# Batch 1's attention in two row parts, and only the unused slots of P's buffers cleared

## The chip, the cores and the metric

The kernel runs on one core of a Trainium2 chip. The metric is the device time of one execution in microseconds (us); of several runs of a kernel the median is given. A core has five engines with queues of their own: TensorE (PE; "PEld" in the profile is its loading of weights), VectorE (DVE), ScalarE (ACT), GpSimd (POOL) and SyncE (SP). SP issues all DMAs of this kernel, in the order of its queue.

## What is computed

Causal attention over 4 batches, 12 heads, 448 tokens and 64 dimensions, all in float32; its output, laid out as 1792 tokens by 768, goes through a multi-layer perceptron (MLP) with a squared ReLU:

```python
def _attn_ref(q, k, v):                     # (4, 12, 448, 64)
    scores = scale * np.matmul(q, k.transpose(0, 1, 3, 2))
    scores = np.where(mask, -1000000000.0, scores)
    scores = scores - np.max(scores, axis=-1, keepdims=True)
    attn = np.exp(scores)
    attn = attn / (np.sum(attn, axis=-1, keepdims=True) + 1e-09)
    return np.matmul(attn, v)

def _moe_ref(x, w_in, w_out):               # (1792, 768), (768, 2048), (2048, 768)
    r = np.maximum(x @ w_in, 0.0)
    return (r * r) @ w_out
```

## The kernel before

**Arithmetic.** The large products run in fp16: each operand is a sum of two fp16 halves, hi and lo, and a product is three fp16 products (hi·hi, hi·lo, lo·hi). The batches 0 and 1 have their scores in float32, the batches 2 and 3 in split fp16.

**Stages.** Batch 0's attention is computed first, while the weights arrive and are split (`early`, in two row parts of 256 and 192 tokens; `weights_in`, `weights_out`). Then, for each batch, `attention(b)` works on six pairs of heads (`pair`), and the MLP on blocks of up to 256 tokens (`sub_block`). Batch 0's MLP has blocks of 256 and 128 tokens; its last 64 tokens go with the first 192 of batch 1 into batch 1's first block (`segs` `[(64, 0), (192, 1)]` in the loop at the end of the kernel), and the following 256 tokens are batch 1's second block.

**A pair.** The rows of a head's scores are cut into four chunks of 112 (`NCH` = 4, `P` = 112); chunk c needs c + 1 chunks of k, so a head has 1 + 2 + 3 + 4 = 10 tiles of 112 x 112. For a pair of batch 1: q and k are loaded (L563, one DMA a head) and v (L567); they are turned on PE (L650) and copied back (L601); the scores are products (L700); VectorE masks and takes the row's maximum (L669), ScalarE takes exp with the sums (L673), VectorE the reciprocals (L710, L713). `halves` writes P's normalised hi (L453) and lo (L466) into the buffer `psrc`, of which there are two, one for each head of the pair. `psrc` has 26 slots of 128 x 128; a slot holds one tile of hi or lo, and six of the 26 hold none. One DMA transpose (L617) turns the 26 blocks into `pt`, from which the values are products (L724, 24 a pair) with v's halves; L736, L737 and L740 write x's hi and lo into `xt`. For batch 1 a copy on GpSimd (L744) brings the 64 tokens of batch 0 along.

**A block.** `sub_block` squares x (L1076, L1079), sums the columns by one product with ones (L1082), makes a power of two for each token from it (L1087 to L1093), rescales x (L1099, three instructions for six pairs), and multiplies with `w_in` (L1139, "L1": 16 groups of 18 products). ReLU, square and halves follow (L1150 to L1157, L453 to L466), then the products with `w_out` (L1176, "L2"), and the output (L1188, L1193, L1197). L1 needs x of all six pairs.

**The order.** Nothing is written in the order in which it runs: each operation is given to a planner (`Plan`) with its reads and writes, its engines (some may run on either of two) and a due time. The due time comes from the table `PR` (a base and a step for each stage, a shift for each kind). `order()` simulates the engines and takes on each the ready operation of the least due time; `elsewhere()` chooses between engines. The engines' queues then run in that fixed order.

**Clearing.** Slots of `psrc` that hold no tile are read by the DMA transpose all the same; `pads` (L1239) clears both buffers whole by GpSimd memsets (L1241) after the last use by batch 0's attention.

Of the kernel before, what the change touches and what calls it, by code (L numbers as in the profile page):

```python
# [1299 lines left out]
```

## Time and profile before

| | us |
|---|---|
| median of 3 runs | 653.37 |
| lowest, highest | 652.10, 654.14 |
| the profiled execution: its own time | 653.86 |
| its span from first to last instruction | 651.8 |
| TensorE's mean granted clock | 0.99 |

| engine | busy, us | share of the span |
|---|---|---|
| PE | 614.0 | 94% |
| DVE | 423.5 | 65% |
| ACT | 415.3 | 64% |
| POOL | 140.4 | 22% |

Times in the rows count from the start of the span. An entry "[2.78 <-DVE xt L1099]" in a timeline says that the engine was idle for 2.78 us before the instruction and what ended that: here a VectorE instruction of line 1099 that wrote xt. The granted clock is a share of TensorE's full 2.4 GHz.

### The profile page before, as it was taken

Reading aid. Unit: us, or ns where it says so; the run is one execution under the profiler, and the core shown is the slowest. Engines: PE = TensorE matmul, PEld = TensorE weight load, DVE = VectorE, ACT = ScalarE, POOL = GpSimd, SP = SyncE. Lnnn points to the kernel's source line nnn. Section 1 sums busy time; section 2 is a strip of 40 time slices with the busy share of each in tenths; the row PEclk is TensorE's granted clock in tenths of the full one; section 3 lists DMA queues with packets and bytes.
Section 4 is the critical chain, followed back from the end, with each engine's and each line's share of the span. In section 5 each row is a group of like instructions: output and inputs, shape, how many; then the busy total and the mean of one; then the engine's idle time right before and its main releaser. Section 6 shows DMA issues by size and latency. Waiting matters only on the chain.

```text
span 651.8 us, 14056 instructions
## 1 busy us (share of the span) xinstructions
PE 614.0 (94%) x5166; PEld 446.6 (69%) x5166; DVE 423.5 (65%) x1263; ACT 415.3 (64%) x1171; POOL 140.4 (22%) x200
## 2 busy tenths in 40 slices
PE   6887999969998996999999999999999999999997
PEld 3553778758664564887767866878768778767764
DVE  3989999999889856779787599885402511401100
ACT  3977999756999975888677799886213233104300
POOL 1000234768300000242004221144012132003300
PEclk9998999999999996999999999999999999999999
DMA  8993574546889897359975989987000000000000
GB/s 217 288 304 123 182 265 166 173 156 165 153 187 205 207 235 175 86 107 197 189 177 110 208 183 204 178 182 141 14 24 14 14 14 13 1 25 13 13 25 24
DMA packets 208771, 87.31 MB, mean 134 GB/s; under 512 B 196160, under 2 KB 203584, under 8 KB 208704
## 3 DMA queue, kind: packets, MB, share of 16 engines
q1 hardware_dynamic: 208704, 86.43, 54.8%
q8 instruction: 40, 0.66, 0.4%
q14 instruction: 27, 0.22, 0.1%
HBM read 45.81 MB, written 5.51 MB: 79 GB/s over the span
## 4 chain that ended last, share of the span: by engine, by line
PE 57%; issue 15%; DVE 14%; ACT 5%; DMA 5%; SPq 3%; POOL 1%; POOLq 0%; ACTq 0%; DVEq 0%
PE bank L1176 25%; PE bank L1139 23%; PE bank L724 3%; PE bank L686 3%; DMA pt<-psrc 2%; DVE wo L929 2%; DVE wo L926 2%; DVE wo L923 2%; SPq L756 1%; DVE bank L814 1%; DMA xt<-in_moe_w_in_dram 1%; DVE wi L929 1%; DMA g<-in_moe_w_in_dram 1%; DVE wi L926 1%; PE bank L938 1%
## 5 line engine op out<-in xcount | busy, mean ns | idle before, releaser
L1139 PE MATMUL bank<-xt,wi 128*128 128x256 f16 (+1 forms) x2304 | 234.7, 261 | 6.1 <-DVE xt L1099 5.2
L1139 PEld LDWEIGHTS <-wi 128*128 128x128 f16 x2304 | 201.7, 98 | 31.9 <-issue 7.7
L1176 PE MATMUL bank<-wo,g 128*128 128x384 f16 x1248 | 212.8, 326 | 0.2 <-DVE wo L466 0.2
L1176 PEld LDWEIGHTS <-g 128*128 128x128 f16 x1248 | 120.4, 98 | 80.4 <-issue 5.0
L461 POOL TENSOR_TENSOR g<-g,g 128x256 f16<-128x256 f32 (+1 forms) x112 | 78.6, 711 | 305.2 <-ACT g L453 174.9
L1152 DVE TENSOR_SCALAR r<-bank 128x256 f32<-128x256 f32 (+1 forms) x96 | 38.1, 400 | 92.5 <-PE bank L1139 61.7
L1157 ACT ACTIVATE g<-r 128x256 f32<-128x256 f32 (+1 forms) x128 | 48.8, 386 | 52.4 <-DVE r L1152 41.0
L673 ACT ACTIVATE pq<-bank,nm 112x336 f32<-112x336 f32 (+3 forms) x144 | 70.7, 508 | 17.0 <-DVE nm L669 10.7
L466 DVE SCALAR_TENSOR_TENSOR psrc<-pq,nm,psrc 112x224 f16<-112x224 f32 (+3 forms) x144 | 71.2, 526 | 5.9 <-ACT psrc L453 5.2
L1193 DVE SCALAR_TENSOR_TENSOR ob<-bank,fac,ob 128x384 f32<-128x384 f32 x26 | 16.0, 615 | 82.6 <-PE bank L1176 82.3
L453 ACT ACTIVATE psrc<-pq,nm 112x224 f16<-112x224 f32 (+3 forms) x144 | 65.3, 545 | 2.9 <-DMA pt<-psrc 2.9
L1188 ACT ACTIVATE ob<-bank,fac 128x384 f32<-128x384 f32 x26 | 15.1, 581 | 74.6 <-PE bank L1176 74.5
L453 ACT ACTIVATE g<-g 128x256 f16<-128x256 f32 (+1 forms) x96 | 36.2, 394 | 32.2 <-PE bank L1176 30.5
L669 DVE CUSTOM_DVE_ANT_0 bank<-bank,mask,sc 112x112 f32<-112x112 f32 (+3 forms) x96 | 46.2, 511 | 7.2 <-PE bank L686 6.1
L455 POOL TENSOR_SCALAR g<-g 128x256 f16<-128x256 f32 x16 | 14.9, 936 | 99.4 <-ACT g L1157 99.4
L686 PE MATMUL bank<-qk 128*112 128x112 f16 (+3 forms) x192 | 33.2, 290 | 3.2 <-DMA qk<-qk 2.9
L673 ACT ACTIVATION_READ_ACCUMULATOR pq<-bank,nm 112x1 f32 x144 | 31.5, 219 | 0.0
L724 PE MATMUL bank<-pt,vp 112*64 112x448 f16 (+3 forms) x432 | 29.9, 284 | 1.0 <-DMA pt<-psrc 0.9
L724 PEld LDWEIGHTS <-vp 112*64 112x64 f16 x432 | 21.8, 110 | 11.5 <-issue 6.1
L686 PEld LDWEIGHTS <-qk 128*112 128x112 f16 x192 | 20.8, 133 | 8.9 <-DMA qk<-qk 3.6
L806 PE MATMUL bank<-wo 64*96 64x256 f32 (+4 forms) x144 | 19.7, 382 | 4.4 <-ACT wo L601 4.3
L814 DVE CUSTOM_DVE_ANT_0 bank<-bank,mask 128x128 f32<-128x128 f32 (+3 forms) x48 | 21.3, 486 | 2.6 <-PE bank L806 2.4
(147 smaller groups left out, 802.0 us busy)
## 6 DMA issues: line engine op xcount, KB each, us to landing
raw<-in_moe_w_out_dram SPq DMA_DIRECT2D x8, 768.0 KB, 4.2
xt<-in_moe_w_out_dram SPq DMA_DIRECT2D x8, 768.0 KB, 4.8
xt<-in_moe_w_in_dram SPq DMA_DIRECT2D x11, 512.0 KB, 6.6
out_dram<-ob SPq DMA_DIRECT2D x26, 192.0 KB, 1.9
raw<-in_moe_w_in_dram SPq DMA_DIRECT2D x9, 512.0 KB, 7.5
vn<-in_v_dram SPq DMA_DIRECT2D x18, 224.0 KB, 3.4
raw<-in_v_dram SPq DMA_DIRECT2D x18, 224.0 KB, 3.1
raw<-in_q_dram SPq DMA_DIRECT2D x12, 224.0 KB, 3.2
```

The costliest lines, as they stand in the source:

```text
L453: nc.scalar.activation(out=o, in_=i, func=ACTF.Copy, scale=s)
L461: return plan.add({"dve": dve_ns(n), "pool": pool2_ns(n)}, lambda e: engines[e].tensor_tensor(out=out(), in0=in_(), in1=top(), op=ALU.subt ...
L466: nc.vector.scalar_tensor_tensor(out=out(), in0=in_(), scalar=scale(), in1=top(), op0=ALU.mult, op1=ALU.subtract)
L669: one("dve", dve_ns(w, 1, 2 if F16S[b] else 1) - 10, lambda e: nc.vector.tensor_tensor_reduce(out=s.ap[0:P, 0:w], in0=s.ap[0:P, 0:w], in1= ...
L673: one("act", act_ns(w, True, 1, True), lambda e: nc.scalar.activation(out=p32[j].ap[0:P, b0 * P:b0 * P + w], in_=s.ap[0:P, 0:w], func=ACTF ...
L686: nc.tensor.matmul(out=s.ap[0:P, 0:(c + 1) * P], lhsT=qT.ap[:, j * NCH + c, :], rhs=kT.ap[:, a:a + c + 1, :].rearrange("p a t -> p (a t)") ...
L724: nc.tensor.matmul(out=pv.ap[j * D:(j + 1) * D, kc * P:S], lhsT=vp.ap[:, hv, vb:vb + D], rhs=pT[j].ap[0:P, hp * NSL + x:hp * NSL + x + w, ...
L814: one("dve", dve_ns(w, 1, 1) - 10, lambda e, c=c, j=j, w=w, ss=ss, nm=nm: nc.vector.tensor_tensor_reduce(out=ss[j].ap[0:M, 0:w], in0=ss[j] ...
L1139: nc.tensor.matmul(out=h.ap[:, 0:n], lhsT=wi_hl(ci, hw)[:, ms], rhs=x[:, kd, hx, off:off + n], start=(kd == 0 and hw == 0 and hx == 0), st ...
L1152: nc.vector.tensor_scalar(out=r.ap[:, 0:n], in0=h.ap[:, 0:n], scalar1=0.0, scalar2=None, op0=ALU.max)
L1157: nc.scalar.activation(out=g32.ap[:, 0:n], in_=r.ap[:, 0:n], func=ACTF.Square)
L1176: nc.tensor.matmul(out=o.ap[:, 0:HALF], lhsT=gv[:, kf, hg, tt * 128:(tt + 1) * 128], rhs=wo_hl(kf, hw)[:, hh * HALF:(hh + 1) * HALF], star ...
```

## The change

1. **Batch 1's attention in two row parts.** `attention(1)` runs twelve jobs in place of six pairs: first all six pairs with the row chunks 0 and 1 (224 rows), then all six with the chunks 2 and 3. Batch 1's first MLP block needs the first part of x alone. The second part has a phase of its own in the table ("f", with F0 and FR). k's chunks 0 and 1 and v's are loaded, turned and split in both parts. A first-part job uses one half of each buffer of P, of `psrc` and of `pt` (by turns), and a DMA transpose of 6 blocks; a second-part job the whole, and 16 blocks (`SLOTS`).
2. **Clearing.** `pads` clears only the slots and the columns that hold nothing, by four ACT copies of zeros (or VectorE memsets) for each of the two buffers. The mask is cleared by VectorE.
3. **The table `PR`** has new values throughout, so that instructions move on every engine.

```diff
-    "B1": -5632767, "B2": -48927, "B3": -8054168, "E0": -8696670, "ER": 17110, "M0": 3904615, "N0": -9012245,
+    "B1": -4814806, "B2": 259207, "B3": -8361854, "E0": -9195508, "ER": 139465, "F0": -2935097, "FR": 16247,
...
-    def pair_load(i):
+    def pair_load(i, cs=tuple(range(NCH))):
         b, pr = divmod(i, NPAIR)
+        c0, c1 = cs[0], cs[-1] + 1
+        phase, at = ("f", 2 * pr) if c0 else ("a", 2 * i)
         for n, a in enumerate((q, k, v)):
             t, keys = raw_of(i)[n]
+            ca = 0 if n else c0
+            nc_ = c1 - ca
...
+    def halves(due, cs, src, skey, rr, rkey, ps, pT, pj):
+        first, step, ns = SLOTS[cs[0], len(cs)]
...
+        one("sp", 19.2 * 2 * ns, lambda e: nc.sync.dma_start_transpose(
+            out=pT.ap[:, 0:2 * ns], in_=ps.ap[0:P, 0:2 * ns].rearrange("p a d -> p (a d)")),
+            [(ps, c, z) for c in cs for z in range(2)] + [("pads", pj)], [pT], due, 260.0 + 125.0 * 2 * ns)
+
+    SLOTS = {(0, NCH): (0, NCH - 1, NSL), (0, 2): (0, 1, 3), (2, 2): (2, 2, 8)}
...
+                chunks = range(c0 * (1 - n), c1)
...
+        z = None if whole or c0 else pr % 2
+        p32, pT, ps = [[mk(j, z) for j in range(2)] for mk in (n_p32, n_pT, n_ps)]
...
         def values16(e):
-            for kc in range(NCH):
-                x, w = 4 * kc, NCH - kc
+            for kc in range(c1):
+                ca = max(kc, c0)
+                x, w = step * kc + ca - first, c1 - ca
...
-        xk = [("xt", b % 2, pr, z) for z in range(3)]
+        xk = [("xt", b % 2, pr, z) for z in ((1, 2) if c0 else (0, 1) if not whole else range(3))]
...
+        if b == 1:
+            jobs = [(i, cs) for cs in ((0, 1), (2, 3)) for i in pairs]
+            for x, job in enumerate(jobs):
+                for n in jobs[x + (x > 0):x + 2]:
+                    pair_load(*n)
+                pair(job[0], None, job[1])
+            return
...
-        nc.gpsimd.memset(mask, 0.0)
+        nc.vector.memset(mask, 0.0)
...
-    def pads(e):
-        for t in psrc:
-            nc.gpsimd.memset(t, 0.0)
+    def pads(e, t):
+        for w in (t[:, :, P:], t[:, 6:15:8, 0:P], t[:, 20:21, 0:P], t[:, 23:25, 0:P]):
+            if e == "act":
+                nc.scalar.activation(out=w, in_=mask[0:P, 0:w.shape[2]].unsqueeze(1).to_broadcast(list(w.shape)), func=ACTF.Copy)
+            else:
+                nc.vector.memset(w, 0.0)
...
-    spare = [plan.spot([("psrc", i, j) for j in range(2)], psrc[i]) for i in range(2)]
-    plan.add({"pool": 2000}, pads, [], spare + ["pads"] + [("psrc", i, c, z) for i in range(2) for c in range(NCH) for z in range(2)],
-             ("a", H, "ld"))
+    for j in range(2):
+        plan.add({"dve": 900, "act": 1250}, lambda e, t=psrc[j][0:P]: pads(e, t), [], [n_ps(j), ("pads", j)], ("a", H, "ld"), "pad", True)
```

In the changed kernel the lines have other numbers: L1210 is L2 (L1176 before), L1116 the column sums (L1082), L1173 L1 (L1139), L731 the fp32 scores (L700), L758 the values (L724), L677 the turning of q and k (L650), L638 the DMA transpose (L617), L579, L585 and L589 the loads (L563, L567), L1283 the clearing.

TensorE where batch 0's MLP ends, before: the last L2 products, the column sums of batch 1's first block, its first L1 products.

```order
L1176 LDWEIGHTS qk
L1176 MATMUL bank_123<-wo,qk 128x384
L1176 LDWEIGHTS qk
L1176 MATMUL bank_123<-wo,qk 128x384
L1082 LDWEIGHTS ones_b
L1082 MATMUL bank_119<-sq,ones_b 128x256
L1139 LDWEIGHTS wi
L1139 MATMUL bank_123<-xt_143,wi 128x256
L1139 LDWEIGHTS wi
L1139 MATMUL bank_123<-xt_143,wi 128x256
```

After, at the same place: the column sums, then work of a second-part job.

```order
L1210 LDWEIGHTS qk
L1210 MATMUL bank_123<-wo,qk 128x384
L677 MATMUL bank_111<-ident,raw 128x112 x4
L1116 LDWEIGHTS ones_b
L1116 MATMUL bank_119<-sq,ones_b 128x256
L731 MATMUL bank_115<-raw 112x336
L731 MATMUL bank_131<-raw 112x336
L731 MATMUL bank_107<-raw 112x448
L731 MATMUL bank_111<-raw 112x448
L758 LDWEIGHTS vp
```

Further on, the first L1 products of the block stand behind the scores of the last second-part job:

```order
L758 LDWEIGHTS vp
L758 MATMUL bank_103<-pt,vp 64x112
L677 MATMUL bank_115<-ident,raw 128x112 x2
L677 MATMUL bank_131<-ident,raw 128x112 x4
L731 MATMUL bank_107<-raw 112x336
L731 MATMUL bank_111<-raw 112x336
L731 MATMUL bank_115<-raw 112x448
L731 MATMUL bank_131<-raw 112x448
L1173 LDWEIGHTS wi
L1173 MATMUL bank_123<-xt_143,wi 128x256
```

What moved: 24 values, turns and scores now stand between the column sums and L1, and L1's first 18 products stand ahead of the values of the last three second-part jobs (two more groups of 24 follow further down, the last one behind 144 products of L1).

SP in batch 1's attention, before: one pair's loads and the two DMA transposes of 26 blocks.

```order
L617 DMA_TRANSPOSE pt<-psrc_145 128x26x112
L617 DMA_TRANSPOSE pt<-psrc_146 128x26x112
L563 DMA raw<-in_q_dram 112x4x64 x2
L563 DMA raw<-in_k_dram 112x4x64 x2
L567 DMA raw<-in_v_dram 112x8x64
L617 DMA_TRANSPOSE pt<-psrc_145 128x26x112
L617 DMA_TRANSPOSE pt<-psrc_146 128x26x112
```

After, in the second part: the transposes have 16 blocks (in the first part 6).

```order
L638 DMA_TRANSPOSE pt<-psrc_145 128x16x112
L638 DMA_TRANSPOSE pt<-psrc_146 128x16x112
L579 DMA raw<-in_q_dram 112x2x64 x2
L579 DMA raw<-in_k_dram 112x4x64 x2
L589 DMA raw<-in_v_dram 112x8x64
L638 DMA_TRANSPOSE pt<-psrc_145 128x16x112
L638 DMA_TRANSPOSE pt<-psrc_146 128x16x112
```

What moved: as many loads stand between two jobs of the second part as stood between two pairs (q's for half the rows, k's and v's for all), and there are six jobs of the first part besides.

The clearing, before, on GpSimd, between the halves of batch 0's MLP:

```order
L455 TENSOR_SCALAR g<-g_1529 128x256
L461 TENSOR_TENSOR g<-g_1529,g 128x256
L1241 MEMSET psrc_145 128x3328
L1241 MEMSET psrc_146 128x3328
L455 TENSOR_SCALAR g<-g_1595 128x256
L455 TENSOR_SCALAR g<-g_1612 128x256
```

After, on ACT; the same four copies for psrc_146 follow some fifteen rows later.

```order
L1191 ACTIVATE g_1478<-r 128x256
L1283 ACTIVATE psrc_145<-mask 112x26x16
L1283 ACTIVATE psrc_145<-mask 112x2x112
L1283 ACTIVATE psrc_145<-mask 112x112
L1283 ACTIVATE psrc_145<-mask 112x2x112
L615 ACTIVATE psrc_146<-psrc_146,nm 96x352 x2
L1184 ACTIVATE r<-bank_119 128x256
L531 ACTIVATE junk,vst<-vn 128x448
```

What moved: the clearing has left GpSimd's queue for ACT's, and it stands before the end of batch 0's attention (L615 is a normalisation of that).

## Rows read from the trace of the kernel before

**Rows 1.** The page: busy us (share of the span) xinstructions of each engine.

```profile
PE 614.0 (94%) x5166; PEld 446.6 (69%) x5166; DVE 423.5 (65%) x1263; ACT 415.3 (64%) x1171; POOL 140.4 (22%) x200
```

**Rows 2.** Windows: in each stretch, busy us of each engine, PEclk, DMA share, GB/s.

```profile
66.00:120.00 54.00, 54.00 (x512) 43.19 (x511) 52.22 (x125) 52.35 (x135) 19.88 (x20) 1.00 0.54 188
120.00:160.00 40.00, 32.95 (x428) 29.14 (x427) 39.76 (x72) 22.62 (x64) 30.89 (x34) 1.00 0.62 188
160.00:245.00 85.00, 80.87 (x623) 48.23 (x621) 70.72 (x223) 78.93 (x227) 8.76 (x19) 1.00 0.89 194
245.00:261.00 16.00, 9.87 (x56) 6.67 (x54) 10.41 (x37) 8.97 (x27) 0.67 (x1) 0.68 0.75 171
```

**Rows 3.** PE's timeline, 241 to 261 us: start, length, engine, line, operands, [idle before <-releaser].

```profile
241.64 4.07 PE L1176 MATMUL bank<-wo,qk 128*128 128x384 f16 x24
245.80 0.27 PE L1082 MATMUL bank<-sq,ones_b 128*128 128x256 bf16 x1
248.85 0.81 PE L1139 MATMUL bank<-xt,wi 128*128 128x256 f16 x6 [2.78 <-DVE xt L1099]
250.46 1.44 PE L1139 MATMUL bank<-xt,wi 128*128 128x256 f16 x6 [0.79 <-DVE xt L1099]
...
256.08 1.09 PE L686 MATMUL bank<-qk 128*112 128x336 f16 x5 [2.30 <-DMA qk<-qk]
256.96 3.51 PE L1139 MATMUL bank<-xt,wi 128*128 128x256 f16 x18
```

**Rows 4.** VectorE's timeline, 248 to 252 us: first and third rescaling.

```profile
248.12 0.68 DVE L1099 TENSOR_TENSOR xt<-xt,sg 128x1024 f16<-128x1024 f16 x1
...
251.32 0.68 DVE L1099 TENSOR_TENSOR xt<-xt,sg 128x1024 f16<-128x1024 f16 x1
```

**Rows 5.** The chain of waits: start, us, engine, what, line, instructions.

```profile
408.95 1.55 PE bank L724 x24
410.50 0.81 PE bank L686 x6
...
530.89 15.72 PE bank L1139 x144
```

**Rows 6.** PE's timeline, 188 us: eight turns of q and k.

```profile
188.05 1.01 PE L650 MATMUL bank<-ident,raw 112*128 112x112 f32 x8
188.89 2.12 PE L1176 MATMUL bank<-wo,g 128*128 128x384 f16 x12
```

**Rows 7.** Timelines of GpSimd, VectorE and PE, 125 to 135 us.

```profile
125.03 5.68 POOL L1241 MEMSET psrc<- 128x3328 f16 x2
...
126.13 4.99 DVE L923 TENSOR_SCALAR wo<-raw 128x768 int32<-128x768 int32 x1
...
134.46 0.55 DVE L923 TENSOR_SCALAR wo<-xt 128x768 int32<-128x768 int32 x1
...
131.23 0.51 PE L1015 MATMUL bank<-wo 128*128 128x128 bf16 x6 [2.23 <-DVE p L478]
```

**Rows 8.** Groups by line and form: ACT's normalisation of 448 columns.

```profile
L593 ACT ACTIVATE psrc<-psrc,nm 96x448 f32<-96x448 f32 x8 | 5.3, 664 | 0.0
```

**Rows 9.** PE's timeline, first and last of five waits in 160 to 240.

```profile
196.70 1.57 PE L700 MATMUL bank<-raw 64*112 64x336 f32 x6 [0.58 <-ACT pq L673]
...
227.87 1.59 PE L724 MATMUL bank<-pt,vp 112*64 112x448 f16 x23 [0.59 <-DMA pt<-psrc]
```

**Rows 10.** SP's timeline: DMA issues, 181 to 248 us.

```profile
181.33 6.37 SPq L617 DMA_TRANSPOSE pt<-psrc  x2
187.75 1.11 SPq L563 DMA_DIRECT2D raw<-in_q_dram  x2
...
246.57 1.23 SPq L636 DMA_TRANSPOSE qk<-qs  x1
```

**Rows 11.** DMA issues: operands, engine, count, KB each, median us to landing.

```profile
raw<-in_q_dram SPq DMA_DIRECT2D x12, 224.0 KB, 3.2
...
raw<-in_q_dram SPq DMA_DIRECT2D x12, 112.0 KB, 2.7
```

More of the change, by code (lines that the diff above doesn't have):

```diff
@@ L61 @@
+    "ws_wn.hi@act": -38135, "ws_wn.hi@dve": 129552, "ws_wn.hi@pool": 72402, "ws_wn.lo@dve": 16397,
+    "ws_wn.lo@pool": 120960, "ws_wn.rest@act": -91715, "ws_wn.rest@dve": 56998, "wt_wn": 1241781,
+    "wt_wn.hi@act": -289805, "wt_wn.hi@dve": 27877, "wt_wn.hi@pool": 117559, "wt_wn.lo@dve": 112951,
+    "wt_wn.lo@pool": -81617,
 }
@@ L404, in attention_relu2_kernel, with n_part @@
     pt = const.tile([128, 2, 2 * NSL * P], F16, name="pt")
-    n_p32 = lambda j: plan.spot([("pq", j, z) for z in range(2)], pq[:, j])
-    n_pT = lambda j: plan.spot([("pt", j, z) for z in range(2)], pt[:, j].rearrange("p (a t) -> p a t", t=P))
+    def n_part(tag, j, z, ap):
+        n = ap.shape[1] // 2
+        return plan.spot([(tag, j, x) for x in range(2) if z in (None, x)], ap if z is None else ap[:, z * n:(z + 1) * n])
+    n_p32 = lambda j, z=None: n_part("pq", j, z, pq[:, j])
+    n_pT = lambda j, z=None: n_part("pt", j, z, pt[:, j].rearrange("p (a t) -> p a t", t=P))
+    n_ps = lambda j, z=None: n_part("psrc", j, z, psrc[j])
     def n_ep(part, j, z):
@@ L679, in pair @@
             for j in range(2):
-                for c in range(NCH):
+                for c in cs:
                     s = n_s(b, 0)
@@ L690, in pair @@
                     one("pe", 2 * mm_ns((c + 1) * P), scores16, [qT, (kT, 0), (kT, 1), (kT, 2)], [s],
-                        ("a", 2 * i + j + 0.05 * c, "sc"))
+                        (phase, at + j + 0.05 * c, "sc"))
                     soft(c, j, s)
         else:
-            for c in range(NCH):
+            for c in cs:
                 ss = [n_s(b, j) for j in range(2)]
@@ L707, in pair @@
         for j in range(2):
-            due = ("a", 2 * i + j, "P")
+            due = (phase, at + j, "P")
             rr = lambda a, z, j=j: f32(nm[j], 4 + a, 4 + z)
             one("dve", 69, lambda e, j=j, rr=rr: nc.vector.tensor_scalar(
-                out=rr(0, NCH), in0=f32(sm[j], 0, NCH), scalar1=1e-9, scalar2=1.0 / PSC, op0=ALU.add, op1=ALU.mult),
-                [(sm[j], c) for c in range(NCH)], [(nm[j], "t")], due, port=True)
-            one("dve", 94, lambda e, rr=rr: nc.vector.reciprocal(out=rr(0, NCH), in_=rr(0, NCH)),
+                out=rr(c0, c1), in0=f32(sm[j], c0, c1), scalar1=1e-9, scalar2=1.0 / PSC, op0=ALU.add, op1=ALU.mult),
+                [(sm[j], c) for c in cs], [(nm[j], "t")], due, port=True)
@@ L714, in pair @@
+            one("dve", 94, lambda e, rr=rr: nc.vector.reciprocal(out=rr(c0, c1), in_=rr(c0, c1)),
                 [(nm[j], "t")], [(nm[j], "r")], due, port=True)
-            halves(n=2 * i + j, src=lambda j=j: p3(j), skey=p32[j], rr=rr, rkey=(nm[j], "r"), pT=pT[j])
+            halves(due, cs, src=lambda j=j: p3(j), skey=p32[j], rr=rr, rkey=(nm[j], "r"), ps=ps[j], pT=pT[j], pj=j)
         pv = n_pv(b)
+        first, step, ns = SLOTS[c0, len(cs)]
+        t0, t1 = c0 * P, c1 * P
         def values16(e):
-            for kc in range(NCH):
-                x, w = 4 * kc, NCH - kc
+            for kc in range(c1):
+                ca = max(kc, c0)
+                x, w = step * kc + ca - first, c1 - ca
@@ L721, in values16 @@
                 for z, (hv, hp) in enumerate(((0, 0), (0, 1), (1, 0))):
                     for j in range(2):
-                        vb = (j * NCH + kc) * D
+                        vb = (j * c1 + kc) * D
                         nc.tensor.matmul(
-                            out=pv.ap[j * D:(j + 1) * D, kc * P:S], lhsT=vp.ap[:, hv, vb:vb + D],
-                            rhs=pT[j].ap[0:P, hp * NSL + x:hp * NSL + x + w, :].rearrange("p a t -> p (a t)"),
-                            start=(kc == 0 and z == 0), stop=(kc == NCH - 1 and z == 2))
@@ L729, in pair @@
-        due = ("a", 2 * i + 1, "val")
-        one("pe", 1550, values16, [(vp, 0), (vp, 1)] + pT, [pv], due, tiled=True)
-        due = ("a", 2 * i + 1, "x")
+                            out=pv.ap[j * D:(j + 1) * D, ca * P:t1], lhsT=vp.ap[:, hv, vb:vb + D],
+                            rhs=pT[j].ap[0:P, hp * ns + x:hp * ns + x + w, :].rearrange("p a t -> p (a t)"),
+                            start=(kc == 0 and z == 0), stop=(kc == c1 - 1 and z == 2))
+        due = (phase, at + 1, "val")
+        one("pe", 3 * sum(mm_ns((c1 - max(kc, c0)) * P) + 10 for kc in range(c1)) + 15, values16, [(vp, 0), (vp, 1)] + pT, [pv], due, tiled=True)
@@ L742, in pair @@
             [pv] + xk, xk, due)
-        if b % 2:
+        if b % 2 and not c0:
             one("pool", pool_ns(128), lambda e: nc.gpsimd.tensor_scalar(
```

113 lines of the change are left out of this document (60 added, 53 removed), and 44 rows, old and new, of tables (LINES, PR).

## The prediction

> **What bounds the kernel now.** I began with the busy shares of the page: TensorE (PE) is busy 94% of the span, the others at most 65% [rows 1]. So the kernel loses time only where PE stands still or runs at half clock, and gains none from work taken off another engine unless PE was waiting for that engine. The second view is the table of stretches [rows 2]. From 66 to 120 us PE is busy 54.00 of 54 us. From 120 to 160 it is busy 32.95 of 40, beside a VectorE (DVE) that is busy 39.76: there DVE is the bound. From 160 to 245, the attention of batch 1, PE is busy 80.87 of 85, ScalarE (ACT) 78.93. From 245 to 261 PE is busy only 9.87 of 16 us, at a mean granted clock of 0.68: for its length the worst of these stretches.
>
> The third view is PE's timeline around that stretch [rows 3]. The last product of batch 0's second MLP half ends at 241.64 + 4.07 = 245.71. Then PE has the column sums for batch 1's first block (L1082, 0.27 us), and 2.78 us of nothing, until VectorE's rescaling (L1099) of that block's x; further waits of 0.79, 0.16 (not shown) and 2.30 us follow, the last one for batch 2's scores. The first 36 products of the block's L1 end at 256.96 + 3.51 = 260.47. VectorE's own timeline shows the chain [rows 4]: the first rescale starts at 248.12 and the third ends at 252.00. Nothing else is ready then: all of batch 0's work is used up, and every product of batch 1 needs this block.
>
> How much is lost? From 245.71 to 260.47 are 14.76 us. At full clock an L1 product costs 15.72 / 144 = 0.109 us, six fp16 scores 0.81 us [rows 5]; 36 products, six scores and the column sums (some 0.1) make 3.93 + 0.81 + 0.1 = 4.85 us. So **9.9 us** are lost, some 6 of them as idle time and the rest by products at half clock (1.2 GHz): L1's first six after the wait take 1.44 us from start to end [rows 3], against 0.65 at full clock.
>
> **The change, part by part.**
>
> *Batch 1 in two row parts.* The first 64 + 192 tokens of the MLP now need only the first 224 rows of batch 1, six jobs that are done before the six jobs of the second part. The order shows what that does: the column sums of the block stand right behind the last product of batch 0, but 24 value products, six transposes and eight fp32 scores of the second part stand between them and the first L1 product; and 144 products of L1 then stand ahead of the last value products. What stands between is about 1.55 us of values [rows 5], 0.6 of transposes (0.105 each, below) and 1.6 to 1.9 of scores, some 4 us, against 2.7 us from the column sums to the end of the first rescale (246.07 to 248.80). In VectorE's order the three rescales stand ahead of the masking of the following scores. So the wait has its cover, the clock has no reason to fall, and batch 0's last MLP work no longer has to fill the wait for batch 1's last values: L1 does. I take back 8.9 us of the 9.9 and leave 1 for the second and third rescale and for batch 2's first scores, whose 2.30 us wait is on their own DMA. Bounds: −9.9 to −7.0. If that cover were gone, the 2.78 us wait would come back first.
>
> *Added PE work.* The first two row chunks of k are transposed twice: 12 more transposes. Eight take 0.84 us from their start at 188.05 to the next instruction [rows 6], 0.105 each: +1.2 us. The value products grow from 24 to 12 + 24 for a pair, 72 more over six pairs, with the same number of columns in all. The trace has no product split this way. Free at one end; at the other each costs the mean 1.55 / 24 = 0.065 [rows 5], +4.7 us. I take +2.0, since the new ones are short ones. Together **+3.2** (+1.2 to +6.0).
>
> *The memsets.* Before, GpSimd clears both psrc buffers whole at 125.03 for 5.68 us; a VectorE instruction that starts beside it takes 4.99 us, and 0.55 for the same shape at 134.46; PE stands idle 2.23 us right after [rows 7]. Now eight ACT copies of zeros clear only the unused slots. By the nearest ACT row, a scaled copy of 448 columns, each costs at most 0.66 us, so at most 5.3 together on ACT [rows 8]. The order also takes 12 of the 48 normalisations of batch 0 from ACT to VectorE (10 rows, two of them double): ACT loses 12 x 0.6 = 7 us of work, VectorE takes on about 12 x 0.55 = 6.6, by its 768-column row [rows 7]. Thus VectorE gets 4.4 us back and some 6.6 more to do. Some of it lies in 66 to 120, where PE had no idle time to lose; some in VectorE's bound stretch. I take **−1.5** (−4.4 to +1.0). The Trainium skill (SBUF — State Buffer, "SBUF: two separate sides") says that a GpSimd instruction and a VectorE one in a two-port mode take the shared port pair as an exclusive lock, the other one waiting for the whole instruction; the 4.99 us agree with that. By this rule alone the 4.4 would all come back in a stretch that VectorE bounds, and the sum would be 2.9 lower.
>
> *Waits inside batch 1's attention.* PE waits five times there, 0.58 + 0.81 + 0.47 + 1.20 + 0.59 = 3.65 us in all, mostly for exp on ACT [rows 9]. Twelve shorter jobs in place of six have twice as many such places, but more MLP work to put between (L1 beside the last three jobs). Between −3.7 (all covered) and +4.0 (as many again) I take **−1.0**, since the same ACT work now spreads over a stretch that is longer by L1's share.
>
> *SP's queue.* SP issues all loads and DMA transposes in order. A transpose of 26 blocks occupies it 6.37 / 2 = 3.2 us, one of 8 blocks 1.23; a plain load 0.55 [rows 10]. On that line a block costs 0.11 and an instruction 0.35: 6 blocks 1.0, 16 blocks 2.1. Twelve of each take 37 us, as twelve of 26 do now. Loads of batch 1 grow from 30 to 66: +20 us at 0.55, in a stretch of some 100 us of which SP then uses about 80. Loads stand one job ahead in the order, so this costs nothing; a 112 KB load lands in 2.7 us and a 224 KB one in 3.2 [rows 11], so halving buys nearly nothing but delays nothing either. If that cover is gone, see the third rival.
>
> The sum: 653.86 (the profiled execution's own time: 651.8 of span and 2.06 outside) − 8.9 + 3.2 − 1.5 − 1.0 = 645.7. The profiled execution is 0.5 above the median of 653.37, so 645.2 for the median.
>
> **The rivals.**
>
> *Lockstep in the longer stretch.* ACT is busy 78.93 of 85 us and VectorE 70.72 in batch 1's attention [rows 2]. In two parts each job's chain (scores, mask, exp, normalise, split, DMA transpose, values) is as deep as before but has half as much work, so PE may wait for it at each of twelve places: +4.0 in place of −1.0, and 2 us more of the stall left: 652.2 on this median. For it: the waits named. Against it: most of each job is covered by MLP products. Chance 0.14; a milder form of it, under 651.4, holds 0.06 of this.
>
> *The stall only moves.* The column sums wait for VectorE's squares, which stand behind the halves of the later jobs; if they come late, PE stops for the same 9.9 us at another place, and 654.1 is left. Against it: x of the first part is complete several jobs earlier. Chance 0.06.
>
> *Slower: SP's issue.* If a DMA transpose costs SP by the instruction rather than by the block, 24 of them cost 24 x 3.2 = 77 us in place of 37, and with 36 us of loads and some 6 of other transfers SP needs 119 us in a stretch of 100; the last values then come about 19 us later than their products can begin, and the time is some 664. It decides from (100 − 42) / 24 = 2.4 us a transpose on. Against it stands the 1.23 us of the 8-block one. Chance 0.08. The Trainium skill (DMA: Bandwidth & Descriptors, "Rules for kernel authors") speaks against the change in the same place: it says to coalesce small transfers, since under 64 KB one pays mostly overhead, and the first part's loads of 224 rows for one head are 57 KB. The rows agree in that the time to landing hardly falls with the size; that it ends on the path, no row shows.
>
> **How the numbers follow.** Chances: the forecast (some 639 to 650) 0.72, lockstep 0.14, the stall moved 0.06, SP 0.08. A measurement of this kernel can tell about 0.3% from no change: below 651.4 is faster, above 655.3 slower. Faster: 0.72 and the 0.06 of mild lockstep, 0.78. Slower: 0.08. The rest, 0.14, is the same. The best ends of all terms at once would give 653.4 − 9.9 + 1.2 − 4.4 − 3.7 = 636.6, which I hold unlikely; the range goes from 638.5 to 653.5, which takes in lockstep and leaves out SP, the moved stall and a little at the low end.
>
> **What would show it.** Right: PE's timeline has the first L1 product of batch 1 behind scores of the second part with under 1 us of idle time, no stretch with a clock below 0.9 between batch 0's last product and batch 2's first scores, no VectorE instruction of 5 us in 120 to 160, 16-block transposes at about 2.1 us of SP. Wrong: PE idle for DMA pt<-psrc or for a rescale in batch 1's part, more than 4 us of waits for exp there, or transposes of 3 us at 16 blocks. It would also be wrong if the whole order, which moved everywhere, lost time in the first 66 us, where batch 0's loads come in another order; I put 2 us on that, inside the range.

## The result and the profile after

The changed kernel takes **647.39 us** (median of 5 runs, 645.31 to 648.71), where the kernel before took 653.47 in the runs beside it: a ratio of 0.9901, 95% interval 0.9875 to 0.9927. The forecast was 645.2, 638.5 to 653.5. The profiled execution has a span of 646.1 us where before it was 651.8. The same kernel, run once more beside the variants below, gave 648.75 and a ratio of 0.9931 (0.9910 to 0.9952), so its gain lies between 4.5 and 6.1 us by the two medians.

The stretches, after (columns as in [rows 2]: us, then busy us of PE, its weight loads, VectorE, ACT and GpSimd, TensorE's granted clock, DMA share, GB/s; the ends are those of the changed kernel's own stages):

```profile
120.00:160.00 40.00, 34.54 (x455) 30.27 (x452) 39.40 (x70) 26.11 (x76) 33.89 (x32) 1.00 0.63 204
160.00:240.00 80.00, 73.82 (x597) 45.55 (x595) 65.04 (x232) 67.49 (x204) 6.56 (x19) 0.99 0.69 155
240.00:261.00 21.00, 20.00 (x185) 15.71 (x184) 18.33 (x61) 18.37 (x47) 2.55 (x3) 0.87 0.90 172
```

Against [rows 2]: PE is busy 34.54 of 40 us in 120 to 160, where it was 32.95. The 16 us at 245 to 261 with PE at 9.87 and a clock of 0.68 are gone; but 240 to 261 still shows a clock of 0.87, and 160 to 240 has PE busy 73.82 of 80, with no other engine near full in the mean of that stretch (VectorE 65.04, ACT 67.49, where ACT had been at 78.93 of 85). At its end it is otherwise:

```profile
232.00:242.00 10.00, 6.36 (x51) 3.76 (x51) 9.83 (x37) 8.67 (x24) 0.00 (x0) 0.83 1.07 190
```

From 232 to 242 us VectorE is busy 9.83 of 10; its timeline marks no wait from 227 to 244.

PE's timeline around the place of the old stall [rows 3]:

```profile
230.49 2.12 PE L1210 MATMUL bank<-wo,qk 128*128 128x384 f16 x12
232.44 0.55 PE L677 MATMUL bank<-ident,raw 112*128 112x112 f32 x4
232.83 0.27 PE L1116 MATMUL bank<-sq,ones_b 128*128 128x256 bf16 x1
233.62 1.57 PE L731 MATMUL bank<-raw 64*112 64x336 f32 x8 [0.52 <-ACT raw L623]
...
236.19 1.17 PE L758 MATMUL bank<-pt,vp 112*64 112x224 f16 x23 [0.78 <-DMA pt<-psrc]
238.42 0.56 PE L677 MATMUL bank<-ident,raw 112*128 112x112 f32 x2 [1.05 <-ACT pq L704]
239.63 1.01 PE L677 MATMUL bank<-ident,raw 112*128 112x112 f32 x4 [0.65 <-ACT pq L704]
241.27 2.96 PE L731 MATMUL bank<-raw 64*112 64x336 f32 x8 [0.63 <-ACT raw L623]
244.16 2.71 PE L1173 MATMUL bank<-xt,wi 128*128 128x256 f16 x18
...
247.93 2.14 PE L1173 MATMUL bank<-xt,wi 128*128 128x256 f16 x18
```

Batch 0's last product ends at 230.49 + 2.12 = 232.6. The column sums are at 232.83, and the first L1 group of batch 1 starts at 244.16, without a wait of its own and behind the scores of the last second-part job, as the order says. But ahead of it PE waits five times in eight microseconds: 0.52, 0.78, 1.05, 0.65 and (at 241.27) 0.63. From the third of these waits on, at some 238.5 us, it runs at half clock, until 245: the six turns take 0.56 and 1.01 us, where others of the same shape took 0.41 (230.24) and 0.55; the eight scores take 2.96, those at 233.62 took 1.57; and the first 18 L1 products 2.71, the next 2.14. VectorE rescales at 240.66, 7.8 us behind the column sums, since four halves and the masks of another job stand ahead:

```profile
237.14 2.23 DVE L477 SCALAR_TENSOR_TENSOR psrc<-pq,nm,psrc 112x336 f16<-112x336 f32 x4
...
240.66 0.69 DVE L1133 TENSOR_TENSOR xt<-xt,sg 128x1024 f16<-128x1024 f16 x1
```

All waits of PE from 160 to 262 us (who waited for what: us in total, times, longest):

```profile
PE bank L677 <- DMA raw<-in_k_dram: 2.8, 2, 1.7
PE bank L677 <- ACT pq L704: 2.1, 3, 1.1
PE bank L731 <- ACT raw L623: 1.2, 2, 0.6
PE bank L758 <- DMA pt<-psrc: 0.8, 1, 0.8
PE bank L1173 <- DVE r L1186: 0.4, 1, 0.4
```

These add up to 7.3 us. The same view of the kernel before adds up to 9.9 in that stretch; 6.0 of them are the stall's (2.78 + 0.79 + 0.16 + 2.30). Over the whole span, by the same view:

| stretch, us | PE's waits before | after |
|---|---|---|
| 0 to 66 | 14.5 | 13.0 |
| 66 to 120 | 0 | 0.4 |
| 120 to 160 | 7.0 | 5.5 |
| 160 to 262 | 9.9 | 7.3 |
| 262 to 460 | 1.4 | 1.9 |
| sum | 32.8 | 28.1 |

So 4.7 us of waits are gone. Of half-clock time, the stall held 9.9 − 6.0 = 3.9 us, and the new place holds 0.6 for the turns, 1.4 for the scores and 0.6 for the products, 2.6: 1.3 less. PE's added work goes against it. Twelve more turns, at 0.10 us each from the start of four to the next instruction (232.44 to 232.83), cost +1.2, as forecast. The values are seen directly, PE's timeline of a first-part job, then of a second-part one:

```profile
175.09 0.63 PE L758 MATMUL bank<-pt,vp 112*64 112x224 f16 x12
175.65 1.15 PE L1210 MATMUL bank<-wo,g 128*128 128x384 f16 x6
...
220.77 1.20 PE L758 MATMUL bank<-pt,vp 112*64 112x224 f16 x24
221.90 0.41 PE L677 MATMUL bank<-ident,raw 112*128 112x112 f32 x2
```

From its start to the next instruction a first-part job's twelve value products take 0.56 us and a second-part job's 24 take 1.13; together 1.69 for a pair, against 1.55 [rows 5], so 0.8 us for six pairs. The sum is −4.7 − 1.3 + 2.0 = −4.0, and the spans differ by 5.7. Of the 1.7 that are left, 1.6 are clock in the first 66 us, where the profiled execution of the kernel before has a mean of 0.97 and that of the changed kernel 1.00. PE's timeline before, then that of pads_on_act (below), a variant of the kernel before that has the same work in the same order there:

```profile
51.27 0.54 PE L980 MATMUL bank<-vn,ones_f 128*128 128x128 f32 x2 [2.40 <-DVE vn L976]
...
55.34 0.28 PE L1082 MATMUL bank<-sq,ones_b 128*128 128x256 bf16 x1
```
```profile
51.55 0.49 PE L980 MATMUL bank<-vn,ones_f 128*128 128x128 f32 x2 [2.36 <-DVE vn L976]
...
53.98 0.28 PE L1082 MATMUL bank<-sq,ones_b 128*128 128x256 bf16 x1
```

Behind the same wait the same work takes 55.34 − 51.27 = 4.07 us in the one and 2.43 in the other, where the clock is 1.00 throughout. So these 1.6 us belong to the execution that was profiled, not to the change.

### The profile page after: what moved, and what is told of

Its sections match the earlier page's. It is cut to its first block, busy times and chain, and to the rows that moved or that the text cites. A ratio compares the mean times of both kernels' runs of the same rounds, so it can differ in the third digit from the quotient of the medians.

```text
span 646.1 us, 14403 instructions
## 1 busy us (share of the span) xinstructions
PE 613.5 (95%) x5250; PEld 448.7 (69%) x5250; DVE 431.2 (67%) x1320; ACT 417.3 (65%) x1191; POOL 126.1 (20%) x181
## 4 chain that ended last, share of the span: by engine, by line
PE 51%; DVE 21%; DMA 10%; ACT 10%; issue 3%; SPq 3%; POOL 3%; DVEq 0%; ACTq 0%; POOLq 0%
PE bank L1210 24%; PE bank L1173 19%; DMA raw<-in_q_dram 3%; DVE psrc L477 3%; PE bank L758 2%; DVE bank L848 2%; ACT pq L704 2%; PE bank L717 2%; DVE wi L963 2%; DVE bank L700 2%; SPq L790 2%; DVE wi L960 1%; PE bank L731 1%; DMA raw<-in_k_dram 1%; POOL qk L466 1%
## 5 line engine op out<-in xcount | busy, mean ns | idle before, releaser
L1173 PE MATMUL bank<-xt,wi 128*128 128x256 f16 (+1 forms) x2304 | 232.8, 260 | 4.0 <-ACT r L1184 2.5
L1173 PEld LDWEIGHTS <-wi 128*128 128x128 f16 x2304 | 201.0, 98 | 28.9 <-issue 4.7
L1210 PE MATMUL bank<-wo,g 128*128 128x384 f16 x1248 | 213.1, 326 | 0.0
L1210 PEld LDWEIGHTS <-g 128*128 128x128 f16 x1248 | 120.5, 98 | 76.1 <-issue 1.0
L472 POOL TENSOR_TENSOR g<-g,g 128x256 f16<-128x256 f32 (+1 forms) x112 | 83.9, 757 | 383.3 <-ACT g L464 294.1
L704 ACT ACTIVATE pq<-bank,nm 112x224 f32<-112x224 f32 (+3 forms) x144 | 69.8, 494 | 17.0 <-DVE nm L700 13.1
L477 DVE SCALAR_TENSOR_TENSOR psrc<-pq,nm,psrc 112x112 f16<-112x112 f32 (+3 forms) x144 | 69.5, 513 | 5.5 <-ACT psrc L464 5.0
L464 ACT ACTIVATE psrc<-pq,nm 112x112 f16<-112x112 f32 (+3 forms) x144 | 66.3, 524 | 6.1 <-DMA pt<-psrc 5.0
L700 DVE CUSTOM_DVE_ANT_0 bank<-bank,mask,sc 112x112 f32<-112x112 f32 (+3 forms) x96 | 46.3, 511 | 5.9 <-PE bank L717 3.7
L758 PEld LDWEIGHTS <-vp 112*64 112x64 f16 x504 | 23.2, 110 | 12.4 <-issue 8.2
L758 PE MATMUL bank<-pt,vp 112*64 112x224 f16 (+3 forms) x504 | 30.7, 268 | 0.8 <-DMA pt<-psrc 0.8
L704 ACT ACTIVATION_READ_ACCUMULATOR pq<-bank,nm 112x1 f32 x144 | 29.4, 204 | 0.0
L700 DVE CUSTOM_DVE_ANT_0 bank<-bank,mask 112x224 f32<-112x224 f32 (+3 forms) x48 | 20.3, 474 | 2.9 <-PE bank L731 2.8
```

The costliest lines, as they stand in the source:

```text
L464: nc.scalar.activation(out=o, in_=i, func=ACTF.Copy, scale=s)
L472: return plan.add({"dve": dve_ns(n), "pool": pool2_ns(n)}, lambda e: engines[e].tensor_tensor(out=out(), in0=in_(), in1=top(), op=ALU.subt ...
L477: nc.vector.scalar_tensor_tensor(out=out(), in0=in_(), scalar=scale(), in1=top(), op0=ALU.mult, op1=ALU.subtract)
L700: one("dve", dve_ns(w, 1, 2 if F16S[b] else 1) - 10, lambda e: nc.vector.tensor_tensor_reduce(out=s.ap[0:P, 0:w], in0=s.ap[0:P, 0:w], in1= ...
L704: one("act", act_ns(w, True, 1, True), lambda e: nc.scalar.activation(out=p32[j].ap[0:P, b0 * P:b0 * P + w], in_=s.ap[0:P, 0:w], func=ACTF ...
L758: nc.tensor.matmul(out=pv.ap[j * D:(j + 1) * D, ca * P:t1], lhsT=vp.ap[:, hv, vb:vb + D], rhs=pT[j].ap[0:P, hp * ns + x:hp * ns + x + w, : ...
```

## The experiments

Theory A, from the forecast: the change wins by the cover that the first block gives to the tail of batch 1's attention, and by the memsets. What remained open after the result was what the new waits at 233 to 241 us are: holes in the order (A), the pace of VectorE or ACT (B), or a cycle of halves, DMA transposes and single buffers (C).

Most variants keep the changed kernel's operations and move a few in the planned order; a diff then shows only the moves. In them 1511 and 1516 are the first two L1 groups of batch 1's first block, 1497 its column sums, 1498 to 1500 the exponent steps and 1501 to 1503 the rescales; 1455 is the turn of q in the last job, 1414 the values of the fourth second-part job, 992 an output step of batch 0.

**The changed kernel again**, for comparison:

> The changed kernel itself, so that the variants of it are compared on one chip and beside the same runs of the kernel before. Expected by every theory: 646 to 648.5, a ratio of 0.988 to 0.993.

648.75 us, ratio 0.9931 (0.9910 to 0.9952), at the edge of what was expected. The two sets of runs of one kernel differ by 1.4 us; a variant that is within 2 us of it is not told apart by one set.

**The cover taken away.** The block's L1 and all that follows from it (but not its sums, rescales and factors) go behind the last x of the second part, operation 1487:

```diff
+    end = spot(1487)
+    late = [s for s in seq[:end] if plan.ops[s[0]][4][0] == "m" and plan.ops[s[0]][4][2] not in ("msq", "sig", "tau", "fac")]
...
+    seq[end + 1:end + 1] = late
```

> The changed kernel with one thing undone: in every engine's order the MLP work of batch 1's first block (L1 and what follows from it) stands behind the last x of the second part, where the changed kernel has 144 of its products ahead of the last values; the rescaling stays where it is. Theory (the gain is the cover of the second part's tail by that block): PE then waits for the values of the last two jobs with nothing to fill, between the scores that ended at 244.2 us and about 258 to 262, some 10 to 15 us and half clock on top, so 657 to 663 against 647.4. Rival (the gain comes from the weights' stretch and from the order elsewhere, the cover is worth little): under 651.

663.26 us, ratio 1.0145 (1.0115 to 1.0175): 10 us slower than the kernel before, 16 slower than the changed one, at the upper end of what the theory of the cover had said. PE's timeline:

```profile
259.08 0.39 PE L758 MATMUL bank<-pt,vp 112*64 112x224 f16 x1 [6.10 <-DMA pt<-psrc]
260.64 2.12 PE L758 MATMUL bank<-pt,vp 112*64 112x224 f16 x23 [1.16 <-DMA pt<-psrc]
262.69 12.56 PE L1173 MATMUL bank<-xt,wi 128*128 128x256 f16 x109
```

PE waits 6.10 and 1.16 us for transposed P, and the first L1 product comes at 262.69, where it was at 244.16. So the part of theory A on the cover holds: without the first block's early start the split itself would cost far more than it gives, since a second-part tail has nothing to hide it. The mean clock from 240 to 261 us is 0.58.

**The clearing, from both sides.** The memsets in the changed kernel, and the ACT copies in the kernel before:

```diff
+        if e == "pool":
+            nc.gpsimd.memset(t, 0.0)
+            return
...
+        after(i, max((last_dep(j) for j in pad), key=spot), "pool")
```

> The changed kernel with only the clearing undone: GpSimd memsets of both buffers in place of the eight ACT copies, behind the same work as before the change; the other engines' orders stay. Theory (the memset holds VectorE up, which bounds that stretch): a VectorE instruction of 4 to 5 us returns near 120 to 130 us, and the time rises by 1.5 to 4.4 us, to 649 to 651.8. Rival (the VectorE time is made up, since later steps wait for something else): within 0.7 us of 647.4.

650.21 us (649.6 to 652.32), ratio 0.9948 (0.9930 to 0.9966): 2.8 above the first set of the changed kernel, and 1.5 above the second, whose interval overlaps. The same run shows what the row parts and the new order give without the new clearing: 3.5 us against the 653.76 of the kernel before beside it.

```diff
-            nc.gpsimd.memset(t, 0.0)
+            for w in (t[0:P, :, P:], t[0:P, 7:21:13, 0:P], t[0:P, 10:12, 0:P], t[0:P, 23:25, 0:P]):
+                nc.scalar.activation(out=w, in_=mask..., func=ACTF.Copy)
```

> The kernel before with the clearing alone changed: eight ACT copies of zeros, of the slots that hold nothing, in place of GpSimd's memsets of both buffers; every other instruction stays in its order. Theory (VectorE was held for 4.4 us by the memset in a stretch that VectorE bounds): the 4.99 us instruction falls to 0.55, PE's wait of 2.23 us at 131 goes, and the time falls by 1.5 to 4.4 us, to 649 to 652. Rival (VectorE's later steps wait for something else, so that the gain is given back before 160 us): within 0.7 us of the kernel before.

651.52 us, ratio 0.9969 (0.9949 to 0.9990): 0.3% or 2.0 us, with an interval from 0.7 to 3.3. In VectorE's timeline the instruction that took 4.99 us [rows 7] now takes:

```profile
130.72 0.55 DVE L923 TENSOR_SCALAR wo<-xt 128x768 int32<-128x768 int32 x1
```

The wait of 2.23 us is gone too. So the clearing is worth about 2 us, a third to under a half of the whole gain, and of the 4.4 us of VectorE's time that come free about half reach the end. In the other direction (memset_back) the size is less certain, since it is clear of one set of the changed kernel and not of the other, and the mechanism was not the one that I had written down. No VectorE instruction of 4 to 5 us returned. GpSimd's timeline there, and PE's wait behind it:

```profile
123.71 6.80 POOL L472 TENSOR_TENSOR g<-g,g 128x256 f16<-128x256 f32 x1
130.45 6.09 POOL L1282 MEMSET psrc<- 112x3328 f16 x2
```
```profile
139.49 0.51 PE L1173 MATMUL bank<-xt,wi 128*128 128x128 f16 x6 [1.80 <-DVE xt L1133]
```

Here a GpSimd subtraction (L472, 757 ns in the mean of those of the changed kernel) took 6.80 us while VectorE worked on without a gap, the memsets followed, and PE waited 1.80 us for a rescale, where the changed kernel waits 1.05. That the one engine or the other is held up for microseconds is shown in both traces, and it is not the same one: before, VectorE's instruction had begun behind the memset (126.13 and 125.03 us); here the subtraction begins amid VectorE's run. That one fully waits for the other is what the Trainium skill says of the two (SBUF — State Buffer, "SBUF: two separate sides"); that GpSimd waited through several VectorE instructions in a row, the rows add.

**k's loads early on SP.**

```diff
+    for i in (1229, 1228, 1268, 1267):        # k of the first two second-part jobs
+        after(i, last_dep(i))
```

> The changed kernel with one change on SP alone: the k loads of the first two jobs of the second part are issued as soon as their buffers are free, ahead of some first-part transposes and output DMAs. Theory (the two waits of PE for k, 1.12 us at 197.9 and 1.67 at 204.5, are SP's queue: the loads stand behind transposes and other loads): both waits go, and the time falls by 1.5 to 2.8 us, to 644.6 to 645.9. Rival (the waits are covered elsewhere: the same PE work then meets ACT's or VectorE's chain later): the waits go, the time stays within 0.7 us of 647.4.

646.26 us, ratio 0.9883 (0.9861 to 0.9905). The waits of PE from 160 to 262 us:

```profile
PE bank L677 <- ACT pq L704: 2.6, 3, 1.4
PE bank L731 <- ACT raw L623: 1.2, 2, 0.7
PE bank L758 <- DMA pt<-psrc: 0.3, 1, 0.3
```

The 2.8 us of waits for k are gone from the list; the median is 1.1 us lower than the changed kernel's, between the two theories, and the intervals overlap. Shown is that the k waits go when SP's order changes; how much of the time comes back is not.

**The holes filled by ready work.**

```diff
+    after(1497, 992)
+    for i in (1503, 1502, 1501, 1500, 1499, 1498):
+        after(i, 1497)
+    before(1511, 1455)
```

> The changed kernel with the column sums of batch 1's first block, their exponent steps and the three rescales (L1116, L1121 to L1127, L1133) placed about 8 us earlier on PE and VectorE, and the first 18 products of L1 ahead of the last job's turns. Theory (the four waits of PE between 233 and 241 us, 3.1 us, and the half clock after them come from the block's rescaling standing behind the masks of the fifth job in VectorE's order, though its sums were ready at 233): a first L1 group fills the waits, PE's loss in 232 to 246 falls from some 5.5 us by 2 to 4, so 643.5 to 645.5. Rival (VectorE and ACT pace the second part, and what is put ahead of the masks delays the scores' banks by as much): 647 to 648.5, the waits only move.

647.70 us, ratio 0.9916 (0.9883 to 0.9949), no gain, though the clock stays at 1.00 from 230 to 262 us: a wait of 1.5 us for transposed P has come instead, where it was 0.8. Together with k's loads and a second group (`before(1516, 1414)`):

> The changed kernel with three moves together: k's loads of the first two second-part jobs early on SP, the first block's column sums and rescales early on PE and VectorE, and two groups of 18 L1 products ahead (one before the last job's turns, one before the values of the job that waited for its DMA transpose). Theory A (PE's losses there are holes that ready work can fill, one by one): the two waits for k (2.8 us) and the waits for exp and for the transposed P fill up, 642 to 645. Theory B (ACT's and VectorE's chain of the second part paces it, and work put ahead of a wait delays that chain by as much): the waits move behind the filled ones, 646 to 648.

646.48 us, ratio 0.9906 (0.9885 to 0.9926), against 648.75 beside it, the intervals overlapping. PE's waits:

```profile
228.06 0.41 PE L677 MATMUL bank<-ident,raw 112*128 112x112 f32 x2 [0.76 <-ACT pq L704]
...
230.92 0.60 PE L677 MATMUL bank<-ident,raw 112*128 112x112 f32 x4 [0.50 <-ACT pq L704]
232.15 1.57 PE L731 MATMUL bank<-raw 64*112 64x336 f32 x8 [0.63 <-ACT raw L623]
...
237.85 0.60 PE L677 MATMUL bank<-ident,raw 112*128 112x112 f32 x4 [0.48 <-ACT pq L704]
239.14 1.57 PE L731 MATMUL bank<-raw 64*112 64x336 f32 x8 [0.69 <-ACT raw L623]
...
245.60 0.38 PE L541 MATMUL bank<-s,ones_f 128*128 128x1 f32 x2 [1.20 <-ACT pq L704]
```

The clock stays at 1.00 from 232 to 262 us, where the changed kernel beside it had 0.89. But the waits are not gone: these six are 4.3 us together, five of them of the same two kinds as before, exp before a turn and a turn's copy before its scores. Ready work put into one hole leaves the next, as theories B and C say.

**Is VectorE the pacer?** v's lo half of five second-part jobs on GpSimd (the operations named are these five):

```diff
+    for i in (1313, 1351, 1389, 1427, 1460):
+        after(i, seq[spot(i) - 1][0], "pool")
```

> The changed kernel with v's lo half of five second-part jobs (0.75 us each on VectorE) done by GpSimd, which is busy 6.6 us of 80 there; PE's order stays. Theory B (VectorE is a pacer of the second part's chain): PE's waits between 228 and 246 us shrink, the time falls by 1 to 3 us. Theory A (the waits come from the order, VectorE has time to spare): within 0.7 us of the changed kernel, or up to 1 us slower where GpSimd's longer step is waited for.

646.08 us, ratio 0.9898 (0.9874 to 0.9922).

```profile
PE bank L677 <- ACT pq L704: 2.6, 3, 1.7
...
PE bank L731 <- ACT raw L623: 1.2, 2, 0.6
```

The median is 2.7 us under the changed kernel's beside it, as theory B has it, but the waits that it should have shortened stand as they were (exp 2.6 us, it was 2.1; the copies 1.2, as before). With overlapping intervals I count it as not told apart. Nor does it free VectorE where the waits are:

```profile
232.00:242.00 10.00, 6.46 (x44) 3.79 (x46) 9.81 (x37) 7.89 (x22) 1.39 (x2) 0.75 1.01 202
```

VectorE is busy 9.81 of 10 us there, as in the changed kernel (9.83). So theory B isn't tested in that stretch, and it stays open.

**Are the buffers of P?** A second pair for every other second-part job, in batch 0's x, which is idle there:

```diff
+        b = plan.spot([("spare", j)], xt[0]...[:, j * 2688:j * 2688 + 2048]...)
...
+        ... n_ps if not c0 or pr % 2 == 0 else lambda j, z: n_ps_spare(j) ...
```

> The changed kernel with a second pair of P buffers for every other job of the second part (in the first x buffer, which is idle there), so that a job's halves needn't wait for the job before to be transposed; every engine's order stays, and pt stays single. Theory C: ACT's waits for pt<-psrc before the halves go (1.08, 0.92, 0.98, 1.10 us at 227 to 244), the transposes start up to 2 us earlier until pt limits them, PE's waits at 236 to 241 shrink, and the time falls by 1 to 3 us, to 645 to 646.5 where the changed kernel gives 647.4 to 648.8. Rival (exps and masks are late for another reason): ACT's waits go, PE's stay, the time within 0.7 us.

647.61 us, ratio 0.9921 (0.9893 to 0.9949). ACT no longer waits for pt<-psrc anywhere from 215 to 250 us, as both sides expected. PE's waits (lines are 5 higher in this kernel):

```profile
235.11 1.57 PE L736 MATMUL bank<-raw 64*112 64x336 f32 x8 [0.52 <-ACT raw L628]
...
237.42 1.17 PE L763 MATMUL bank<-pt,vp 112*64 112x224 f16 x23 [0.52 <-DMA pt<-psrc]
239.91 0.41 PE L682 MATMUL bank<-ident,raw 112*128 112x112 f32 x2 [1.32 <-ACT pq L709]
241.12 0.62 PE L682 MATMUL bank<-ident,raw 112*128 112x112 f32 x4 [0.80 <-ACT pq L709]
242.42 2.96 PE L736 MATMUL bank<-raw 64*112 64x336 f32 x8 [0.68 <-ACT raw L628]
```

They are 0.52, 0.52, 1.32, 0.80 and 0.68 us, 3.8 in all where it was 3.6 (the profiled execution took 651.48, the longest of this variant's). That the buffers of P alone make these waits falls with it. The same buffers with the three moves of fill_more:

> The second pair of P buffers together with the three moves of fill_more (k's loads early, the block's sums and rescales early, two groups of L1 products ahead). Theory C: with the cycle relaxed, filled holes stay filled, 642 to 645. Rival (the chain still paces): no better than fill_more, 645.5 to 647.5.

645.14 us (643.95 to 646.34), ratio 0.9875 (0.9840 to 0.9909), the lowest of all, 2.5 us under psrc_two beside it, and between what theory C and its rival had said. From 230 to 262 us the clock is 1.00, and no wait for transposed P is left. The three moves with v's lo half on GpSimd:

> The three moves of fill_more together with v's lo half of five second-part jobs on GpSimd; nothing else is changed. If the two gains add (each some 2 us against the changed kernel in the runs beside it), 643 to 645.5, a ratio of 0.984 to 0.988. If they fill the same holes, 645.5 to 647, no better than either.

647.60 us, ratio 0.9926 (0.9903 to 0.9949). The gains did not add. No variant is shown to be faster than the changed kernel: the ratios of those that only fill, reorder or add buffers lie between 0.9875 and 0.9926, and the two sets of the changed kernel itself reach from 0.9875 to 0.9952 with their intervals. psrc_two_moves comes nearest: its interval lies below that of the second set, and overlaps that of the first.

**The transposes made longer**, 24 blocks in place of 16 in the second part (six more slots are cleared for it):

```diff
-            out=pT.ap[:, 0:2 * ns], in_=ps.ap[0:P, 0:2 * ns]...
+            out=pT.ap[:, 0:ns * 3 if ns == 8 else 2 * ns], in_=ps.ap[0:P, 0:ns * 3 if ns == 8 else 2 * ns]...
```

> The changed kernel with the twelve DMA transposes of the second part made longer, 24 blocks in place of 16 (the eight more are read and written and used by nobody; six more slots are cleared for it); every engine's order stays. Theory C (the second part runs in a cycle: DMA transpose of a job, its landing, the halves of the next job into the same psrc, the next transpose; PE's waits from 228 us on are that cycle's): each transpose holds SP 0.9 us longer and lands later, a cycle with two of them grows by 1 to 2 us, and with some four cycles before L1 covers them the time rises by 3 to 7 us, to 650 to 655. Rival (ACT's exps or the order pace it, the transposes are covered): within 1 us of the changed kernel, 646.5 to 649.5.

658.64 us, ratio 1.0078 (1.0049 to 1.0108): some 10 us above the changed kernel, more than the 3 to 7 that I expected. PE's timeline, and one pair of transposes on SP (each one's time as shortest/middle/longest in ns):

```profile
221.83 1.17 PE L758 MATMUL bank<-pt,vp 112*64 112x224 f16 x23 [1.74 <-DMA pt<-psrc]
...
240.63 2.09 PE L758 MATMUL bank<-pt,vp 112*64 112x224 f16 x23 [2.51 <-DMA pt<-psrc]
```
```profile
L638 SPq DMA_TRANSPOSE pt<-psrc x2: 3045/3190/3334, 232.5 to 235.9; - x2
```

Each of the twelve takes 2.8 to 3.3 us of SP here, where ten of the twelve of 16 blocks took 1.45 to 1.61; that is some 1.5 us more, and 0.9 was expected. PE's waits for transposed P grow from 0.8 to 6.4 us, and it falls to half clock again. So the transposes of the second part stand just short of the path: their present length is covered, and of the some 18 us that are added on SP some 10 come out at the end. That is theory C's cycle, as a bound that is close. Whether SP's time or the longer transfers do it (the DMA share from 230 to 262 us is 1.00, where the changed kernel has 0.93) is not shown.

**What remains.** At 233 to 241 us the rows show one job's steps in a row: turn (232.44), its copy on ACT, scores (233.62), masks, exps, and the next job's turns at 238.42 and 239.63, which wait for a bank that the exps free. No MLP product is left to stand between, since batch 0's ended at 232.6 and batch 1's was put behind. Whether this latency makes the waits, or the pace of VectorE, which never waits there and has the block's own exponent steps (L1121 to L1144, 1.9 us) ahead of the masks, stays open: P's buffers alone were tried and are not it, VectorE was not relieved at that place, and a variant with more banks wasn't tried. Untried too is the new table by itself: how much of the 3.5 us that come without the clearing is the table's and not the row parts' was not measured.

## Why the prediction was right, point by point

- **The stall.** Its mechanism was right: the first block starts behind second-part work, without a wait of its own, and covers the tail (no_cover). Its size was the step that failed. "I take back 8.9 us of the 9.9 and leave 1" compared the work between the sums and L1 (4 us) with the rescaling's own 2.7 us, and did not ask what PE waits for inside those 4 us. They took 11.3: some 5 of work (the eight scores are sixteen rows of the trace, and cost 3.0 us, not 1.6 to 1.9), five waits of 3.6 us and 2.6 us of half clock. Waits and clock together, the stretch from 160 to 262 us gave back 2.6 + 1.3 = 3.9 us, where this term and the next stood at 9.9.
- **Waits inside batch 1's attention.** −1.0 was forecast. The old waits before 240 us (3.65) went but for 0.35, and 2.79 us for k's loads came, a term that I had at nothing ("Loads stand one job ahead in the order, so this costs nothing"). The order does have them ahead, but SP reaches them late: between the transposes they wait for those. That was the SP rival's place, with a smaller price.
- **Added PE work.** +3.2 forecast, +2.0 measured: turns +1.2 as said, values +0.8 instead of +2.0.
- **The memsets.** −1.5 forecast; −2.0 in the kernel before, and −1.5 or −2.8 in the changed one, by its set. The order of size was right; the rule of the lock by itself, 4.4, was too much, since half is given back.
- **SP's issue.** 16 blocks were put at 2.1 us and 6 at 1.0. SP's issues in the changed kernel (shortest/middle/longest in ns), one of 6 blocks and two pairs of 16:

```profile
L638 SPq DMA_TRANSPOSE pt<-psrc x1: 1218/1218/1218, 192.1 to 192.1; - x1
L638 SPq DMA_TRANSPOSE pt<-psrc x2: 1568/1588/1608, 230.3 to 232.1; - x2
L638 SPq DMA_TRANSPOSE pt<-psrc x2: 1485/2332/3179, 238.4 to 240.0; - x2
```

Those of 6 blocks take 1.20 to 1.56, ten of the twelve of 16 take 1.45 to 1.61, the other two 2.22 and 3.18. So the line through 8 and 26 blocks does not hold between them: 6 cost more than it says, 16 less. It is not the cost by the instruction either, and the slower rival did not come. The point from which it would decide, put at 2.4 us a transpose, is not contradicted: at 2.8 to 3.3 (long_transpose) the kernel is 5 us slower than before.
- **Lockstep** came in part: around the scores of the last two jobs, not at twelve places, some 4 us in all.
- **Elsewhere.** The first 66 us lost 1.5 us less (13.0 of waits, 14.5 before); I had put ±2 there. The second set of the changed kernel has 13.9 there. The 1.6 us of clock come on top in the profiled executions.
- **The signs.** As forecast: the first L1 product behind scores and without a wait, and VectorE's 5 us instruction gone. Against the forecast: the clock is at half from 238.5 to 245 us, before batch 2's first scores, and PE waited 0.78 us for pt<-psrc, which I had named a sign of being wrong.

The spans differ by 5.7 us where the sum had 8.2: the stall and the attention's waits gave 6.0 less, and 0.9 of new waits came at 66 to 120 and 262 to 460; against that stand 1.2 from the values, and 1.5 of waits and 1.6 of clock from the first 66 us. So that the time came out 2.2 to 3.6 us from the forecast is luck in part: the largest term was some 6 too large, and what made up for more than half of that was the values, which were put too dear, and the first 66 us, which stood in no term.

## What to carry to other kernels

When a stall is to be covered by other work, list the waits inside that work too: cover that itself consists of a chain (turn, copy, scores, mask, exp) is worth its products, not its place in the order. Splitting a stage to let the next begin early pays only as far as the next stage's work is actually interleaved with the split stage's tail; without that, here, it costs 10 us. Clear only what nobody writes, and not on GpSimd beside a stretch that VectorE bounds; on ACT it cost nothing that these runs show.
